# Six V blocks loaded in pairs: three 8 MB transfers with 64 KB rows, and fixed slots for K and V in a decode attention kernel

## The chip, the cores and the metric

The kernel runs on one core of a Trainium2 chip. The core has a matrix engine (PE, with its weight loads shown apart as PEld), VectorE (DVE), ScalarE (ACT), GpSimd (POOL) and SyncE (SP), which here only issues transfers. Sixteen DMA engines move data from the chip's main memory into the on-chip memory of 128 partitions; matrix products go to a second on-chip memory, PSUM, of eight banks. The metric is the device time of one execution in microseconds, lower is better.

## The reference

A batch of 8 tokens x (576 wide) goes through two branches, mixed by a gate g:

```python
g = sigmoid((x * gate_w).sum(-1, keepdims=True))
q = (x @ wq) as 32 heads of 128
k, v = last 2048 of 8192 keys of the caches, 16 heads, each used by 2 query heads
a = softmax(q k^T / sqrt(128)) v @ wo
b = gelu(layernorm(x) @ w1 + b1) @ w2 + b2
out = g * a + (1 - g) * b
```

All inputs are bf16. The part of the caches that is read is 8 x 16 x 2048 x 128 values for K and as many for V, 67 MB each; the weights add 20 MB. Each value is used for two query rows only, so there is little arithmetic per byte.

## The kernel before

**Units.** K and V are cut into 16 units of 4 MB each, n = 4g + i. A unit holds 32 of the 128 (batch, head) pairs (group g) and 512 of their 2048 keys (step i). On chip a unit is 128 partitions of one row of 32 KB: a pair j fills four partitions x, each with 128 keys. Since softmax doesn't ask for an order of keys, any assignment will do as long as K and V have the same.

**A K unit** (`k_unit`) is handled in four quarters: VectorE transposes a quarter in blocks of 32 x 32 (line 694, "tr", into one of two halves of KT), and PE multiplies it with the block-diagonal queries (line 712, "qk", eight matmuls into PSUM banks 0 to 3; all but every fourth are issued through the helper at line 175, so they are listed there). Bank 0 to 3 hold the mask before that, written by ScalarE (line 655). After the last quarter, `softmax` takes the maximum on VectorE (645, "mx"), turns it into the running bias ("nb", 647 or 649), and ScalarE takes the exponential (651) into P. `spread` transposes P on VectorE (669, "pt").

**A V unit** (`v_item`) copies the transposed P into a zeroed block-diagonal array, the spread P (743 on ScalarE and 744 on POOL, two copies each; "px"). PE multiplies it with V in 64 matmuls of 256 columns ("pv", lines 757 and 186, a loop with address registers), and VectorE adds the result to O with the correction for the new maximum ("o", 798 or 800). After each group of four units, VectorE and PE fold O into the final sums (803 to 811). There is one home for the spread P, so the copies for unit n wait until the product of unit n-1 has read it; the last unit uses KT, cleared by POOL (727).

**Transfers.** All large loads are issued by SP, in one order. The 32 KB slots of each partition are four and are taken in turn (1, 2, 0, 3) by the stream K0 K1 V0 K2 V1 K3 ... V14 V15 and then by w2 and wo. A load waits on SP until the slot's last user is done: for a K unit its four transposes, for a V unit its product. At the start wq lies in slot 0, w1 from slot 3 on. At the end come the bias, two thirds of w2, wo in two pieces and the rest of w2, accumulated by PE into the output bank.

**Order.** Every operation is put into a graph with `deps` (real waits on semaphores) and `after` (order of start only). A planner (`_Plan.schedule`) gives each operation a time from its `cost` and writes a fixed order for each engine; transfers follow a rate `DMA_BW` and a latency `DMA_LAT`. `keep_warm` is a filler: matmuls with zeros into a bank that is rewritten later.

The lines around the transfer and the product of a V unit:

```python
def take_slot():
    n = n_slot[0]
    n_slot[0] += 1
    return (1, 2, 0, 3)[n % ND]
...
deps = [d, o_u] + px_done[n] + [o_done.get(n - 2)]
after = pv_hist[-1:] + [qk_unit.get(n + 1)]
```

Of the kernel before, what the change touches and what calls it, by code (L numbers as in the profile page):

```python
# [6 lines left out]
BF = mybir.dt.bfloat16  # L7
F32 = mybir.dt.float32
# [30 lines left out]
class _Plan:  # L39

    DMA_BW = 428e3
    DMA_LAT = 1.8
    DMA_ISSUE = 0.35
# [18 lines left out]
    def schedule(self):  # L62
# [14 lines left out]
        while ready:  # L77
# [18 lines left out]
            if op.is_dma:  # L96
                eng_free[op.eng] = est + op.cost
                if op.nbytes < 65536:
                    op.t1 = est + 0.4 + self.DMA_LAT
# [93 lines left out]
def build_kernel(nc, A_x, A_k_cache, A_v_cache, A_wq, A_wo, B_x, B_w1, B_b1, B_w2, B_b2, gate_w, out):  # L193
# [12 lines left out]
    ND = 4  # L206
# [10 lines left out]
    JN = D // NJ  # L217
    BIG = 1.0e9
    x2 = A_x.rearrange("b s d -> (b s) d")
    out2 = out.rearrange("b s d -> (b s) d")  # L220

    with ExitStack() as es:
# [14 lines left out]
        req("ident", 128, BF)  # L237
        req("ones_bf", 512, BF)
        req("zeros_bf", 128, BF)
# [12 lines left out]
        req("maskhd", 4, F32)  # L252
        req("r8", 128, F32)
        req("idf8", 8, F32)
        req("dg", 16, F32)
        req("sel", 4 * 128, BF)
        req("sel4", 128, BF)
        req("cols", 16, F32)
        req("xT", 6 * 32, BF)
        req("yT", 6 * 32, BF)  # L260
        req("q4", 4 * 256, BF)
        req("qbd", 4 * 4 * 128, BF)
        req("b2", D, BF)
        req("uh", FCW, F32)
        req("v1", FCW, F32)
        req("hT", FT * 32, BF)
# [5 lines left out]
        req("gcol", 1, F32)  # L272
        req("on", 512, BF)
        req("O", 256, F32)
        req("EW", 512, F32)
        req("EV", 128, F32)
        req("oT", 512, BF)
        req("out_sb", JN, BF)
# [4 lines left out]
        over("vm", "uh", 0, 256, F32)  # L283
        over("x_sb", "PT", 0, D, BF)
# [76 lines left out]
        def slot(s):  # L361
            return RAW[:, s * DE:(s + 1) * DE]
# [226 lines left out]

        stream = [("K", 0), ("K", 1)]  # L590
        for vi in range(NL):
            stream.append(("V", vi))
            if vi + 2 < NL:
                stream.append(("K", vi + 2))
        HEAD = 2
# [10 lines left out]
        slot_free = [[o_qp], [], [], [o_hp]]  # L606
        o_px0 = add("pool", lambda e: e.memset(ptx_f, 0.0), deps=[o_qp, o_hp], name="ptx0", cost=4.5)
        n_slot = [0]
        tr_hist, qk_half = [], []
        qk_unit, qb_done = {}, {}  # L610
        pt_done, px_done, pv_done = {}, {-1: [o_px0]}, {}
        ex_done, nb_done, al_done, ss_done, o_done = {}, {}, {}, {}, {}
# [5 lines left out]
        def take_slot():  # L618
            n = n_slot[0]
            n_slot[0] += 1  # L620
            return (1, 2, 0, 3)[n % ND]

        def load_item(cache, nm, n):
            s = take_slot()
            g, i = divmod(n, 4)
            src = cache.rearrange("b h s d -> (b h) s d")[32 * g:32 * g + 32, S0 + KL * i:S0 + KL * i + KL, :].rearrange("j (x r) d -> j x (r d)", x=4)
            d = dma("sp", lambda e: e.dma_start(slot(s), src), "s%d" % s, 8 * W * Dh * 2, deps=slot_free[s], name="%s%d" % (nm, n), after=last_dma[-1:])
            last_dma.append(d)
            slot_free[s] = []
            return s, d  # L630

# [54 lines left out]
        def k_unit(n, s, d):  # L686
            g, i = divmod(n, 4)
            trs = []
            for rh in range(2):
                for hh in range(2):  # L690
                    m = 4 * n + 2 * rh + hh
                    kb = m % 2
                    deps = [d] + ([qk_half[m - 2]] if m >= 2 else [o_selp])
                    tr = add("dve", (lambda rh=rh, hh=hh, kb=kb: lambda e: e.transpose(bass.AP(arena_f, offset=foffs("KT") + kb * 2048, ap=[[AST // 2, 128], [1, 2048]]),  # L694
                                                                                      bass.AP(arena_f, offset=foffs("RAW") + s * SE + rh * (SE // 2) + 32 * hh, ap=[[AST // 2, 128], [64, 64], [1, 32]])))(),
                             deps=deps, name="tr%d_%d%d" % (n, rh, hh), cost=2.3, after=tr_hist[-1:] + ([mx_done.get(n - 1)] if rh + hh == 0 else []) + ([pt_done.get(n - 1)] if rh == 1 and n < NL - 1 else []))
# [4 lines left out]
                    if (rh, hh) == ((1, 1) if n == NL - 1 else (1, 0)):  # L701
# [13 lines left out]
                    if rh == 0 and hh == 0:  # L715
                        deps += qb_done[g] + [mask_done[n]]
                    qk = add("pe", qk_fn, deps=deps, name="qk%d_%d%d" % (n, rh, hh), cost=1.85, after=qk_half[-1:] + pv_hist[-1:])
                    qk_half.append(qk)
            qk_unit[n] = qk
            if n > 4 and n % 4 == 1:  # L720
# [3 lines left out]
            if n == NL - 1:  # L724
                o_kz.deps.append(qk)

        o_kz = add("pool", lambda e: e.memset(view("KT").bitcast(F32), 0.0), deps=[], name="ktx0", cost=4.5, prio=3)  # L727

        def v_item(n):
            s, d = load_item(A_v_cache, "dv", n)  # L730
            g, i = divmod(n, 4)
            if n == NL - 1:
                spread(n)
            ob_ = BK_OS[n % 2]
            px_at = aoffs("KT") if n == NL - 1 else PX
            px_free = [o_kz] if n == NL - 1 else [pv_done.get(n - 1), o_px0]
            px_done[n] = []
            for c in range(4):
                def fn(e, c=c):
                    dst = bass.AP(arena, offset=32 * c * AST + px_at + 32 * c, ap=[[AST, 32], [128, 64], [1, 32]])  # L740
                    src = bass.AP(arena, offset=32 * c * AST + aoffs("PT") + 2048 * (n % 2), ap=[[AST, 32], [32, 64], [1, 32]])
                    if px_engs[n][c] == "act":
                        return e.activation(out=dst, in_=src, func=ACTF.Copy)  # L743
                    return e.tensor_copy(dst, src)  # L744
                px_done[n].append(add(px_engs[n][c], fn, deps=[pt_done[n]] + px_free, name="qrx%d_%d" % (n, c), cost={"act": 1.8, "dve": 0.8, "pool": 2.4}[px_engs[n][c]], prio=5))

            if n == NL - 2:
                mx_done[n + 1].after.extend(op for op in px_done[n] if op.eng == "dve")
                o_kz.deps.extend(op for op in px_done[n] if op.eng == "dve")

# [30 lines left out]
            deps = [d, o_u] + px_done[n] + [o_done.get(n - 2)]  # L781
            after = pv_hist[-1:] + [qk_unit.get(n + 1)]
            if n >= NL - 2:
                after.append(keep_warm("warm_pv%d" % n, (10, 6)[n - NL], after, (ob_,), [o_u, o_done[n - 2]]))
            if n < NL - 1:
                pv = add("pe", lambda e: pv_looped(e, 64, 2, 6 if n < NL - 2 else 12), deps=deps, name="pv%d" % n, cost=8.2, after=after)
            else:
                pva = add("pe", lambda e: pv_looped(e, 48, 4, 14), deps=deps, name="pv%da" % n, cost=5.4, after=after)
# [4 lines left out]
            slot_free[s] = [pv]  # L793
            al = sm[:, n, 3:4]
# [77 lines left out]
        def k_item(n):  # L872
            s, d = load_item(A_k_cache, "dk", n)
            k_unit(n, s, d)

# [9 lines left out]
        for kind, i in stream:  # L885
            {"K": k_item, "V": v_item, "W": wo_all, "M": m2_chunk, "B": bias}[kind](i)

# [63 lines left out]
```

## Time and profile before

| | |
|---|---|
| median of 3 runs | 364.5 us (364.47 to 364.72) |
| profiled execution | 364.57 us, span 363.3 us |
| busy | PE 284.4 us (78%), VectorE 257.3 (71%), ScalarE 131.8 (36%), POOL 73.5 (20%) |
| read from main memory | 154.31 MB, mean 425 GB/s over the span |
| granted PE clock, mean | 0.92 |
| K and V loads | 32 of 4 MB, 26.4 us from issue to landing (median) |
| transposes of K (694) | 64 of 2288 ns |
| maximum (645), transposed P (669), exponential (651), mask (655) | 16 of 2292, 16 of 2274, 16 of 1967, 15 of 1873 ns |
| copies into the spread P | 28 of 1884 ns on POOL, 30 of 1906 ns on ScalarE, 6 of 686 ns on VectorE |

The page gives the busy time of each engine as a share of the span, the span in 40 slices, the transfers, the chain of work that ended last and the costliest groups of instructions by line. The busy share of PE is modelled from pipelined matmuls and includes fillers. In the views in order of time, a row has start, busy time, engine, line, operation, operands and, in brackets, the idle time before it with what ended it. A line of SP marked L627 is the issue of a K or V load.

### The profile page before, as it was taken

To read this page: it belongs to the slowest core of one execution; us is meant where nothing else is said; L and a number is where in the kernel's file an instruction comes from. 1 tells how busy PE (TensorE), PEld (TensorE's weight loads), DVE (VectorE), ACT (ScalarE), POOL (GpSimd) and SP (SyncE) were. 2 spreads that over 40 slices of the span, in tenths; PEclk is the share of its full clock that TensorE was granted. 3 is DMA by queue.
4 is the path that set the end of the run, shared out by engine and by line. 5 is a ranking of instruction groups with operands and counts; after the bars stand their busy time and mean duration, and the time that the engine had idled before them with its cause. 6 is when DMAs were issued, how large, how long until landed. Compare 5 with 4: busy or idle time off the path is not lost.

```text
span 363.3 us, 4428 instructions
## 1 busy us (share of the span) xinstructions
PE 284.4 (78%) x1842; PEld 126.6 (35%) x1381; DVE 257.3 (71%) x201; ACT 131.8 (36%) x117; POOL 73.5 (20%) x72
## 2 busy tenths in 40 slices
PE   0355554999897967997978949897969679978996
PEld 0110000436171703452432607170706034513763
DVE  0722978797978596959495878677695979498530
ACT  1012106274544440735342434444444416313300
POOL 9123002230414040302212030404040403003000
PEclk9976596999998997999896998998999899999999
DMA  8999999999999999999999999999999999999995
GB/s 349 433 440 402 462 404 459 404 462 404 462 404 460 404 462 408 456 411 451 413 451 415 451 415 451 415 451 413 447 419 451 415 451 412 449 415 447 412 440 234
DMA packets 6146, 154.45 MB, mean 425 GB/s; under 512 B 716, under 2 KB 884, under 8 KB 1272
## 3 DMA queue, kind: packets, MB, share of 16 engines
q1 hardware_dynamic: 6080, 154.29, 98.7%
q8 instruction: 6, 0.10, 0.1%
q10 hardware_dynamic: 56, 0.03, 0.0%
q14 instruction: 4, 0.03, 0.0%
HBM read 154.31 MB, written 0.01 MB: 425 GB/s over the span
## 4 chain that ended last, share of the span: by engine, by line
DMA 50%; DVE 35%; PE 9%; issue 4%; ACT 2%; ACTq 0%; POOL 0%; SPq 0%
DMA arena<-in_A_k_cache_dram 42%; DVE arena L694 20%; DMA arena<-in_B_w_dram 5%; DVE arena L669 5%; PE ps L175 4%; DMA arena<-in_gate_w_dram 2%; DVE arena L645 2%; PE ps L186 2%; DVE arena L803 1%; PE ps L505 1%; PE ps L712 1%; DVE arena L800 1%; DVE arena L566 1%; DVE arena L808 1%; ACT arena L651 1%
## 5 line engine op out<-in xcount | busy, mean ns | idle before, releaser
L694 DVE STREAM_TRANSPOSE arena<-arena 128x2048 f32<-128x2048 f32 x64 | 145.0, 2288 | 23.6 <-DMA arena<-in_A_k_cache_dram 20.9
L175 PE MATMUL ps<-arena 128*128 128x512 bf16 (+2 forms) x461 | 131.2, 436 | 0.0
L186 PE MATMUL ps<-arena 128*128 x942 | 106.1, 274 | 0.1
L712 PE MATMUL ps<-arena 128*128 128x512 bf16 x128 | 54.6, 426 | 54.4 <-DVE arena L694 47.7
L186 PEld LDWEIGHTS ps<-arena 128*128 x942 | 92.4, 98 | 11.6 <-issue 0.6
L744 POOL COPY arena<-arena 32x2048 bf16<-32x2048 bf16 x28 | 52.8, 1884 | 211.1 <-DVE arena L669 210.3
L743 ACT ACTIVATE arena<-arena 32x2048 bf16<-32x2048 bf16 x30 | 57.2, 1906 | 64.3 <-DVE arena L669 64.0
L651 ACT ACTIVATE arena<-ps,arena 128x2048 bf16<-128x2048 f32 x16 | 31.5, 1967 | 113.1 <-DVE arena L649 78.5
L712 PEld LDWEIGHTS ps<-arena 128*128 128x128 bf16 x128 | 13.5, 105 | 159.0 <-DVE arena L694 98.1
L645 DVE TENSOR_REDUCE arena<-ps 128x1 f32<-128x2048 f32 x16 | 36.7, 2292 | 35.4 <-PE ps L175 35.4
L669 DVE STREAM_TRANSPOSE arena<-arena 128x2048 bf16<-128x2048 bf16 x16 | 36.4, 2274 | 2.1 <-ACT arena L651 2.1
L655 ACT ACTIVATE ps<-arena 128x2048 f32<-128x2048 f32 x15 | 28.1, 1873 | 0.1
L757 PE MATMUL ps<-arena 128*128 128x256 bf16 x82 | 14.5, 276 | 1.0 <-DVE arena L744 1.0
L757 PEld LDWEIGHTS ps<-arena 128*128 128x128 bf16 x82 | 8.0, 100 | 19.0 <-issue 17.1
L455 PE MATMUL ps<-arena 8*128 8x8 bf16 x8 | 0.6, 171 | 14.6 <-DVE arena L429 9.5
L583 PE MATMUL ps<-arena 128*8 128x288 bf16 (+1 forms) x140 | 9.6, 286 | 1.6 <-DMA arena<-in_A_wo_dram 0.6
L561 DVE TENSOR_TENSOR arena<-arena 128x1152 f32<-128x1152 f32 x1 | 1.4, 1358 | 11.5 <-ACT arena L559 11.5
L727 POOL MEMSET arena<- 128x4096 f32 x1 | 3.5, 3510 | 22.7 <-DVE arena L744 22.7
L583 PEld LDWEIGHTS ps<-arena 128*8 128x8 bf16 (+1 forms) x140 | 5.7, 86 | 5.9 <-DMA arena<-in_B_w_dram 1.3
L638 POOL COPY arena<-arena 32x128 bf16<-32x128 bf16 x16 | 4.6, 287 | 15.0 <-ACT arena L540 7.4
L429 DVE COPY arena<-arena 8x64 bf16<-8x64 bf16 x2 | 0.3, 190 | 9.1 <-DMA arena<-in_gate_w_dram 9.1
L800 DVE SCALAR_TENSOR_TENSOR arena<-arena,ps 128x256 f32<-128x256 f32 x12 | 5.3, 446 | 1.4 <-PE ps L757 1.4
(106 smaller groups left out, 98.9 us busy)
## 6 DMA issues: line engine op xcount, KB each, us to landing
arena<-in_A_k_cache_dram SPq DMA_DIRECT2D x16, 4096.0 KB, 26.4
arena<-in_A_v_cache_dram SPq DMA_DIRECT2D x16, 4096.0 KB, 26.3
arena<-in_B_w_dram SPq DMA_DIRECT2D x1, 4608.0 KB, 23.3
arena<-in_A_wo_dram SPq DMA_DIRECT2D x2, 2304.0 KB, 20.6
arena<-in_A_wq_dram SPq DMA_DIRECT2D x1, 4096.0 KB, 12.9
arena<-in_B_w_dram SPq DMA_DIRECT2D x1, 3456.0 KB, 26.6
arena<-in_B_w_dram SPq DMA_DIRECT2D x1, 1152.0 KB, 19.6
arena<-in_B_w_dram SPq DMA_DIRECT2D x1, 576.0 KB, 24.2
```

The costliest lines, as they stand in the source:

```text
L175: return e.add_instruction(mybir.InstMatmult(name=nc.get_next_instruction_name(), engine=mybir.EngineType.PE, ins=[e.lower_ap(rhs), e.lowe ...
L186: return e.add_instruction(mybir.InstMatmult(name=nc.get_next_instruction_name(), engine=mybir.EngineType.PE, ins=[operand(r, r_ap), opera ...
L583: ins = e.matmul(ps[32 * j:32 * j + 8, BK_ACC, 0:JN], lhsT, rhs[:, JN * j:JN * j + JN], start=False, stop=True, skip_group_check=True, til ...
L645: mx = mx_done[n] = add("dve", lambda e: e.tensor_reduce(out=k(n, MX), in_=ps[:, 0:4, :].rearrange("p a n -> p (a n)"), axis=AXL.X, op=ALU ...
L651: ex = add("act", lambda e: e.activation(out=Pm, in_=ps[:, 0:4, :].rearrange("p a n -> p (a n)"), func=ACTF.Exp, bias=k(n, NB), scale=SCAL ...
L655: mask_done[n + 1] = add("act", lambda e: e.activation(out=ps[:, 0:4, :].rearrange("p a (n c) -> p (a n) c", c=32), in_=bass.AP(arena_f, o ...
L669: pt_done[n] = add("dve", lambda e: e.transpose(bass.AP(arena, offset=aoffs("PT") + 2048 * (n % 2), ap=[[AST, 128], [1, 2048]]), Pm), deps ...
L694: tr = add("dve", (lambda rh=rh, hh=hh, kb=kb: lambda e: e.transpose(bass.AP(arena_f, offset=foffs("KT") + kb * 2048, ap=[[AST // 2, 128], ...
L712: mm = e.matmul(*args, start=False, stop=True, skip_group_check=True) if rc == 0 else held_matmul(nc, e, *args, stop=True, skip=True)
L743: return e.activation(out=dst, in_=src, func=ACTF.Copy)
L744: return e.tensor_copy(dst, src)
L757: mm = e.matmul(ps[:, ob_, 0:256], lhsT, rhs, start=(k == 0), stop=True, skip_group_check=True)
```

## The change

1. The stream is written out: K0 K1 V0 K2 V1 K3 V2 K4 V3 K5 K6 P4 K7 K8 P6 K9 K10 P8 K11 K12 V10 V11 K13 V12 K14 V13 K15 V14 V15. P4, P6 and P8 load V4 with V5, V6 with V7 and V8 with V9 in one transfer of 8 MB, with 64 KB for each partition. For that, units 2m and 2m+1 share a stretch of 1024 keys, 256 to a partition, and each takes one half of the 256. A single load, K or V, still has rows of 32 KB, which now lie 64 KB apart within one pair.
2. K uses slot 1 for even units and slot 0 for odd ones, V slot 2 for even and 3 for odd ones; a pair fills 2 and 3 and waits until both are free. The loads after the stream take slots 1, 0 and 2.
3. The spread P has two homes, the old one and PXB (which the gelu's temporaries use before), each cleared once by POOL; a copy for unit n waits for the product of n-2. KT is not used for it any more. Small arrays are laid over others to make room.
4. In the K unit after the second of a pair's (6, 8, 10, and 15 as before) P of the unit before is transposed after all four quarters instead of after the second. The product of a pair's first V unit comes after the scores of unit n+2 instead of n+1.
5. Ahead of the scores of units 6, 8 and 10 PE runs a filler of 16 matmuls with zeros, written as a loop.
6. The product loops of the last two V units have bodies of 6 instead of 12 and 14 matmuls; the planner's numbers are changed.

```diff
-    DMA_BW = 428e3
-    DMA_LAT = 1.8
+    DMA_BW = 433.2e3
+    DMA_LAT = 0.45
+    DMA_START = 1.7
...
-                    start = max(est + 0.4, dma_free)
+                    start = max(est + self.DMA_START, dma_free)
...
+    STREAM = "K0 K1 V0 K2 V1 K3 V2 K4 V3 K5 K6 P4 K7 K8 P6 K9 K10 P8 K11 K12 V10 V11 K13 V12 K14 V13 K15 V14 V15"
...
+        req("PXB", SE, BF)
+        over("uh", "PXB", 0, FCW, F32)
+        over("v1", "PXB", 4 * FCW, FCW, F32)
...
-        ptx_f = bass.AP(arena_f, offset=PX // 2, ap=[[AST // 2, 128], [1, 4096]])
+        PXS = (PX, aoffs("PXB"))
...
+        px_zero = [add("pool", (lambda k=k: lambda e: e.memset(bass.AP(arena_f, offset=PXS[k] // 2, ap=[[AST // 2, 128], [1, 4096]]), 0.0))(), deps=[o_qp, o_hp] + [o_hf] * k, name="ptx%d" % k, cost=4.5) for k in range(2)]
+        late_slots = [1, 0, 2]
+        pairs = [int(k[1:]) for k in STREAM.split() if k[0] == "P"]
+        late_turn = [n + 2 for n in pairs] + [NL - 1]
...
-        def load_item(cache, nm, n):
-            s = take_slot()
+        def load_item(cache, nm, n, s, both=False):
             g, i = divmod(n, 4)
-            src = cache.rearrange("b h s d -> (b h) s d")[32 * g:32 * g + 32, S0 + KL * i:S0 + KL * i + KL, :].rearrange("j (x r) d -> j x (r d)", x=4)
+            keys = cache.rearrange("b h s d -> (b h) s d")[32 * g:32 * g + 32, S0 + 2 * KL * (i // 2):S0 + 2 * KL * (i // 2) + 2 * KL, :]
+            if both:
+                src, dst = keys.rearrange("j (x r) d -> j x (r d)", x=4), RAW[:, s * DE:(s + 2) * DE]
+            else:
+                src, dst = keys.rearrange("j (x u r) d -> u j x (r d)", x=4, u=2)[n % 2], slot(s)
+            free = slot_free[s] + (slot_free[s + 1] if both else [])
...
-                    if n and (rh, hh) == ((1, 1) if n == NL - 1 else (0, 1)):
+                    if n and (rh, hh) == ((1, 1) if n in late_turn else (0, 1)):
                         spread(n - 1, after=[tr])
+                    if (rh, hh) == (0, 1) and n - 3 in pairs and n - 3 in o_done:
+                        o_done[n - 3].after.append(tr)
...
+                        if n - 2 in pairs:
+                            qk_half.append(keep_warm("warm_qk%d" % n, 16, qk_half[-1:] + pv_hist[-1:], (BK_OS[n % 2],), [o_u, nb_done[n - 1], o_done[n - 4]], looped=True))
...
+        def v_pair(n):
+            d = load_item(A_v_cache, "dv", n, 2, both=True)
+            for u in range(2):
+                v_unit(n + u, 2 + u, d)
...
-            px_at = aoffs("KT") if n == NL - 1 else PX
-            px_free = [o_kz] if n == NL - 1 else [pv_done.get(n - 1), o_px0]
+            px_at = PXS[n % 2]
+            px_free = [pv_done.get(n - 2), px_zero[n % 2]]
...
-            after = pv_hist[-1:] + [qk_unit.get(n + 1)]
+            after = pv_hist[-1:] + [qk_unit.get(n + 2 if n in pairs else n + 1)]
...
-                pv = add("pe", lambda e: pv_looped(e, 64, 2, 6 if n < NL - 2 else 12), deps=deps, name="pv%d" % n, cost=8.2, after=after)
+                pv = add("pe", lambda e: pv_looped(e, 64, 2, 6), deps=deps, name="pv%d" % n, cost=7.1, after=after)
...
-        def keep_warm(name, n, after, banks=(0, 1, 2, 3), deps=None):
+        def keep_warm(name, n, after, banks=(0, 1, 2, 3), deps=None, looped=False):
             def fn(e):
                 mm = None
+                if looped:
+                    args = (ps[:, banks[0], :], zeros_bf, maskR)
+                    e.matmul(*args, start=True, stop=True, skip_group_check=True)
+                    with e.Fori(0, n - 2):
+                        held_matmul(nc, e, *args, start=True, stop=True, skip=True)
+                    return held_matmul(nc, e, *args, start=True, stop=True, skip=True)
...
         def k_item(n):
-            s, d = load_item(A_k_cache, "dk", n)
-            k_unit(n, s, d)
+            s = 1 - n % 2
+            k_unit(n, s, load_item(A_k_cache, "dk", n, s))
```

More of the change, by code (lines that the diff above doesn't have):

```diff
@@ L237, in build_kernel @@
         req("ident", 128, BF)
-        req("ones_bf", 512, BF)
+        req("EW", 512, F32)
+        over("ones_bf", "EW", 0, 512, BF)
+        over("sel", "EW", 1024, 4 * 128, BF)
         req("zeros_bf", 128, BF)
@@ L252, in build_kernel @@
         req("maskhd", 4, F32)
-        req("r8", 128, F32)
         req("idf8", 8, F32)
         req("dg", 16, F32)
-        req("sel", 4 * 128, BF)
         req("sel4", 128, BF)
         req("cols", 16, F32)
-        req("xT", 6 * 32, BF)
-        req("yT", 6 * 32, BF)
+        req("early", 640, BF)
+        over("xT", "early", 0, 6 * 32, BF)
+        over("yT", "early", 384, 6 * 32, BF)
+        over("r8", "early", 768, 128, F32)
+        over("b2", "early", 0, D, BF)
         req("q4", 4 * 256, BF)
         req("qbd", 4 * 4 * 128, BF)
-        req("b2", D, BF)
-        req("uh", FCW, F32)
-        req("v1", FCW, F32)
+        req("vm", 256, F32)
+        req("PXB", SE, BF)
+        over("uh", "PXB", 0, FCW, F32)
+        over("v1", "PXB", 4 * FCW, FCW, F32)
         req("hT", FT * 32, BF)
@@ L282, in build_kernel @@
         req("RAW", ND * DE + SE, BF, 512)
-        over("vm", "uh", 0, 256, F32)
+        over("on", "P", 0, 512, BF)
+        over("oT", "P", 1024, 512, BF)
+        over("out_sb", "PT", 0, JN, BF)
         over("x_sb", "PT", 0, D, BF)
@@ L587, in __init__ @@
                 acc_groups.append(self)
[L590 to L594, printed above, removed]
+        stream = [(k[0], int(k[1:])) for k in STREAM.split()]
         HEAD = 2
@@ L618, in take_slot @@
         def take_slot():
[L619 to L627 removed]
+            return late_slots.pop(0)
+        def load_item(cache, nm, n, s, both=False):
+            g, i = divmod(n, 4)
+            keys = cache.rearrange("b h s d -> (b h) s d")[32 * g:32 * g + 32, S0 + 2 * KL * (i // 2):S0 + 2 * KL * (i // 2) + 2 * KL, :]
[4 more added lines that the diff above has]
+            free = slot_free[s] + (slot_free[s + 1] if both else [])
+            d = dma("sp", lambda e: e.dma_start(dst, src), "s%d" % s, (1 + both) * 8 * W * Dh * 2, deps=free, name="%s%d" % (nm, n), after=last_dma[-1:])
             last_dma.append(d)
             slot_free[s] = []
[L630 removed]
+            if both:
+                slot_free[s + 1] = []
+            return d
         def query(g):
@@ L716, in k_unit @@
                         deps += qb_done[g] + [mask_done[n]]
-                    qk = add("pe", qk_fn, deps=deps, name="qk%d_%d%d" % (n, rh, hh), cost=1.85, after=qk_half[-1:] + pv_hist[-1:])
+                        if n - 2 in pairs:
+                            qk_half.append(keep_warm("warm_qk%d" % n, 16, qk_half[-1:] + pv_hist[-1:], (BK_OS[n % 2],), [o_u, nb_done[n - 1], o_done[n - 4]], looped=True))
+                    qk = add("pe", qk_fn, deps=deps, name="qk%d_%d%d" % (n, rh, hh), cost=1.75, after=qk_half[-1:] + pv_hist[-1:])
                     qk_half.append(qk)
+                    kt_free.append(qk)
             qk_unit[n] = qk
-            if n > 4 and n % 4 == 1:
+            if n > 4 and n % 4 == 1 and (n - 5) // 4 in us_done:
                 us_done[(n - 5) // 4].after.append(qk)
```

33 lines of the change are left out of this document (12 added, 21 removed).

## The prediction

> **What bounds the kernel now.** I read the page first (span, slices, chain), then the stretches between two arrivals of K, then the waits of SP, which issues every large transfer, then SP, PE and VectorE in order of time around K5 and K6.
>
> ```profile
> span 363.3 us, 4428 instructions
> ...
> DMA  8999999999999999999999999999999999999995
> ...
> HBM read 154.31 MB, written 0.01 MB: 425 GB/s over the span
> ...
> DMA 50%; DVE 35%; PE 9%; issue 4%; ACT 2%; ACTq 0%; POOL 0%; SPq 0%
> ```
>
> The DMA engines are full in every slice but the first and the last. The chain names VectorE for 35%, but that is the way back from one arrival of K to the instruction that issued a transfer. Whether the engines ever run dry is seen between arrivals of K (start and end, length, PE busy, granted clock, DMA share, GB/s):
>
> ```profile
> 124.50:163.20 38.70, 31.40 (x191) 0.91 1.00 433
> 163.20:201.90 38.70, 32.83 (x184) 0.87 1.00 433
> 201.90:240.60 38.70, 32.90 (x209) 0.96 1.00 433
> ...
> 344.00:355.00 11.00, 10.28 (x114) 1.00 1.00 427
> ```
>
> And what SP waited for (us in total, times, longest):
>
> ```profile
> SPq L627 <- DVE arena L694: 114.8, 12, 17.3
> ...
> SPq L898 <- DMA out_dram<-arena: 1.1, 1, 1.1
> ```
>
> Four transfers of 4.19 MB take 38.7 us at share 1.00 and 433 GB/s. SP waits a lot (a K transpose, L694, frees a slot), yet nobody behind it starves: a transfer lands 26.4 us after its issue (page, last part) and needs 9.7 of its own, so it was queued some 16.7 us early. So the time is: about 1 us until the first byte, 154.3 MB at 433 GB/s (356.4 us), some 2 us of slack at start and in the 430s of single stretches, 3.7 us from the last landing (359.6) to the end (363.3), and 1.3 us outside the span (the profiled execution took 364.57; the median of the runs is 364.5). No byte is taken away by the change. It can only gain through a higher rate, and lose through an empty DMA queue. The sum is therefore a list of deadlines for SP's issues.
>
> The last row above is SP's only wait for a transfer into an idle queue: 0.32 us of issue and 1.1 of wait, 1.42 us from issue to landing for 4.5 KB. I use it as the price of a start from an empty queue.
>
> **The work around the first pair, as it runs now.** PE in order of time (the bracket is the idle time before, and who ended it):
>
> ```profile
> 133.47 0.40 PE L712 MATMUL ps<-arena 128*128 128x512 bf16 x1 [2.41 <-DVE arena L694]
> ...
> 138.85 0.61 PE L712 MATMUL ps<-arena 128*128 128x512 bf16 x1 [2.99 <-DVE arena L694]
> ...
> 142.84 0.38 PE L757 MATMUL ps<-arena 128*128 128x256 bf16 x2
> ...
> 149.82 0.39 PE L712 MATMUL ps<-arena 128*128 128x512 bf16 x1
> ```
>
> VectorE, then SP, then the clock of that stretch:
>
> ```profile
> 142.18 2.29 DVE L645 TENSOR_REDUCE arena<-ps 128x1 f32<-128x2048 f32 x1 [3.39 <-PE ps L175]
> ...
> 151.82 2.31 DVE L694 STREAM_TRANSPOSE arena<-arena 128x2048 f32<-128x2048 f32 x1 [0.55 <-PE ps L175]
> ```
>
> ```profile
> 126.41 0.54 SPq L627 DMA_DIRECT2D arena<-in_A_v_cache_dram  x1
> ```
>
> ```profile
> 130.00:140.00 10.00, 4.59 (x16) 0.74 1.02 439
> ```
>
> Read off: one V unit holds PE 6.98 us (142.84 to 149.82), and its slot is reissued 7.18 us after its first matmul (119.23 to 126.41). A quarter of scores holds PE 1.80 us (149.82 to the next at 151.62), and the transpose that waits for it starts 2.0 us after the quarter's start (149.82, 151.82). Transposes follow each other every 2.2 us. The granted clock fell to 0.74 over 130 to 140, after idle gaps of 2.41 and 2.99 us, and the quarter at 138.85 took 3.1 instead of 1.8.
>
> **Part by part.** *Rows of 64 KB.* Each of 16 engines moves 8 rows per 4 MB; six units go from 48 rows to 24. Price per row: wo's rows of 18 KB ran at 427 GB/s in the stretch above, K and V at 433 with 32 KB; a fixed cost that explains it is 22 ns per row (18,432 B at 26.69 B/ns is 691 ns, 32,768 at 27.06 is 1,211; the line through both meets zero bytes at 22), so 24 x 22 = 0.5 us gained at most. The stretch 345 to 355, with the same rows of 18 KB, shows 433, so the other end is 0. I take 0.1, near the second, since edges cut a stretch by whole packets. The K rows stay at 32 KB, now 64 KB apart within a head; a head's stride stays 2 MiB, so I cost this at nothing.
>
> *Slots.* K has slots 1 and 0, V has 2 and 3. The order up to K5 is unchanged, so times up to K5's arrival (124.52) can be kept. Arrivals after it, at 9.70 us each (318.46 minus 124.52 is 193.94 for 20 transfers): K6 134.2, P4 153.6, K7 163.3, K8 173.0, P6 192.4, K10 211.8. A transfer costs nothing if issued 1.42 us before its predecessor lands. K2 now waits for K0's transposes (50.42; deadline about 54), P4 for PV of V3 (126.41; deadline 132.8), K8 for K6's transposes (155.2 below; deadline 161.9). They hold by 3.5, 6.4 and 6.7 us. P6 and P8, which need both V slots, are left.
>
> *P6.* Deadline 171.6 (K8 lands 173.0). Start at VectorE's maximum of K5, as now 142.18 to 144.47, bias 144.66. K6 landed at 134.2, so its first two transposes run as in the trace, 144.6 to 149.0. The new filler, 16 matmuls, starts at 144.66 and takes 3.7 us (nine took 2.10 us at 329.44), to 148.4; the mask of K6, on ScalarE as now, is written at 148.7, and covers it. Today K6's scores waited for the PV of V4 until 149.82; that PV now comes later. Quarter one 148.75; third transpose 150.75, fourth 152.95 to 155.15; last quarter 155.2; PV of V4 at 157.0 (P4 landed 153.6, its spread P is old). P of V5 is transposed 155.15 to 157.4 and copied by POOL and ScalarE (two each, 1.9 us a copy) until 161.3, into its second home; PV of V5 starts at 164.0, so it is not held. Slot 3 is free and P6 issued at 164.0 + 7.2 = 171.2. That is 0.4 us inside the deadline: cost 0.
>
> *P8.* Deadline 210.4 (K10 lands 211.8). K7's scores stand behind both PV on PE: 171.0; third transpose 173.0, the update of O 0.4, fourth 175.6 to 177.8, last quarter 177.85, maximum 179.9 to 182.2, exponential and mask 4.0 after 182.5 (161.25 to 165.26 in the trace) to 186.5, the filler meanwhile from 182.35 to 186.1; K8's quarters and transposes 186.5, 188.5, 190.7, 192.95; PV of V6 194.75 (P6 landed 192.4), PV of V7 201.75, P8 issued 208.9: 1.5 us inside. V10 needs only the PV of P8's first half, and its own start is two K loads after P8's landing (231.2), so it has 19 us for 7. What each wait holds up: behind P6 on SP are K9 and K10, due 19 us later.
>
> *The rest.* The three fillers hide under the mask; without that cover each costs 3.7 us on PE. POOL clears two homes for P (3.51 us each) early and no longer clears KT at 332.20: POOL has 290 us idle, and the last PV waits for VectorE's copies (339.07 on), not for it: 0. Bodies of 6 instead of 12 and 14 in the last two PV loops: 60 matmuls took 6.71 us in the one form and 6.72 in the other: 0. Tail: the M2 slot now comes from K14 (earlier), wo's first from K15 as before, its second from V14 as before (issued 339.9, and it is queued behind 8 us of w2): 0. Fewer waits for spread P: 0, since DMA sets the pace.
>
> Sum: 364.57 - 0.1 + 0 = 364.47 for a profiled execution, and 0.07 less for a median: 364.4 us.
>
> **A rule weighed.** The granted clock of K6's quarters decides P6. In the trace it dropped after gaps of 2.41 and 2.99 us. The Trainium skill, "TensorE: Matmul & The Clock Gate", section on what is actually happening, says that half rate comes after at least one idle window of about 3.4 us; by that rule the 1.8 to 2.7 us of idle PE ahead of the fillers would never halve the clock, and the sum would be 364.4. The trace differs (2.99 us, clock 0.74) and decides: by it the first rival's 366.7 is open too.
>
> **Rivals.** *P6 starts late (slower).* The slack is 0.4 us in a chain of 47 us. If the filler runs at half clock (a matmul of 512 columns then takes 0.42 us, four in 1.68 from 138.85), it lasts 6.7 us to 151.4 instead of 148.4, K6's first quarter moves from 148.75 to 151.4, and P6 is issued at 173.85: 2.25 us of empty engines, 366.7. The same ahead of K8 adds 2.65 - 1.5 = 1.2: 367.9. It decides from 0.4 us on; at 1.2 it is over the bound. For it: the measured drop, and a chain with no idle time. Against it: PE was back at full clock from 142 on in the trace, just before the filler. Chance 0.33.
>
> *The long rows pay (faster).* 22 ns per row, 0.5 us: 364.0, and with half a microsecond more from fewer completions or instruction fetches under 363.8. Against it: share 1.00 at 433 in every stretch. Chance of more than 0.2%: 0.08.
>
> *The address pattern costs rate (slower).* Rows of 64 KB keep each engine longer in one place, and the heads lie 2 MiB apart. At 427 instead of 433 GB/s, the slowest stretch, 25.2 MB cost 58.9 instead of 58.1 us: 365.2. The trace shows the 2 MiB stride at the full 433 with rows of 32 KB. Chance 0.04. The Trainium skill, "DMA: Bandwidth & Descriptors", section on latency and other measured facts, gives 164 GB/s for a row pitch of 2 MiB; estimated from that page, 25.2 MB would take 153 us. The trace (433 at that pitch) does not agree, so it moves no chance.
>
> *The change does nothing that shows* is my forecast, 0.55.
>
> **How the numbers follow.** This kernel's runs agree within 0.25 us, so 0.2% (0.7 us) is what a measurement can tell. Forecast 364.4; its own range is 364.0 (rows at their best) to 365.2 (P6 0.8 late). Low 363.9. The rival's 366.7 has most of what is slower, so high is 367.0; some 0.1 lies above and under 0.1 below. Faster 0.08, same 0.55, slower 0.37 (0.33 + 0.04).
>
> **What the profile after would show.** Right: share 1.00 and 433 GB/s across 165 to 215, P6 issued near 171 and P8 near 209, last landing near 359.5, PV of V4 and V5 back to back on PE. Wrong: a dip in the GB/s slice at 171 to 175, with SP released by PE after 171.6; L175 matmuls of the filler at 0.42 us; K7 arriving on time but K9 late by the same amount as P6. If the share stays 1.00 and the time still moves, the rate of 64 KB rows is the cause.

## The result, and the profile after

The changed kernel takes 370.6 us (median of 6 runs, 367.96 to 372.05) against 364.5 (364.38 to 364.72): a ratio of 1.0161, 95% interval 1.0143 to 1.0178. It is slower, by 6 us, above the top of my range (367.0). The spread of its runs grew from 0.3 us to 4. The profiled execution took 370.06 us.

The page of the kernel after:

```profile
span 368.8 us, 4559 instructions
...
DMA  8999999999999999998999999999999999999994
...
HBM read 154.31 MB, written 0.01 MB: 418 GB/s over the span
...
DVE 42%; PE 36%; DMA 14%; ACT 4%; issue 3%; ACTq 0%; POOL 0%; SPq 0%
```

The bytes are the same, the rate over the span fell from 425 to 418 GB/s, one slice in the middle fell from 9 to 8, and in the chain the DMA engines gave way to PE (9% to 36%). So the transfers had waited for the arithmetic. Where, the same stretches show (start and end, length, PE busy, granted clock, DMA share, GB/s):

```profile
124.50:163.20 38.70, 30.35 (x148) 0.96 1.00 433
163.20:201.90 38.70, 33.89 (x204) 1.00 0.97 409
201.90:240.60 38.70, 31.78 (x180) 1.00 0.97 409
240.60:279.50 38.90, 34.22 (x231) 0.96 1.00 433
279.50:318.50 39.00, 32.83 (x201) 0.96 1.00 433
```

At 409 instead of 433 GB/s a stretch of 38.7 us loses 38.7 x (1 - 409/433) = 2.15 us. Two such stretches make 4.3 of the 5.5 us by which the span grew. Outside them the rate is the old one, with rows of 64 KB as with rows of 32. The rest is at the end: the same length of time, 3.8 us before the end of the span, in the kernel after and then in the one before:

```profile
340.00:365.00 25.00, 23.50 (x243) 1.00 0.94 402
```

```profile
334.50:359.50 25.00, 22.82 (x239) 1.00 0.98 418
```

That is 25 x 16/433 = 0.9 us more. The issues of the two pairs, on SP:

```profile
171.19 0.54 SPq L631 DMA_DIRECT2D arena<-in_A_v_cache_dram  x1
...
210.60 0.54 SPq L631 DMA_DIRECT2D arena<-in_A_v_cache_dram  x1
```

P6 was issued at 171.19; the prediction worked out 171.2. It was still late: the engines ran dry around it, as a short stretch of the kernel after shows (the last column is GB/s). P8 was issued 1.7 us after the 208.9 worked out.

```profile
171.00:172.00 1.00, 1.00 (x7) 1.00 0.08 33
```

PE around the filler ahead of K6, in order of time (line 176 is the helper that was 175, 720 the scores, 838 the filler's first matmul, 770 and 187 a product):

```profile
143.36 0.39 PE L838 MATMUL ps<-arena 128*128 128x512 bf16 x1 [1.72 <-DVE arena L655]
143.59 5.22 PE L176 MATMUL ps<-arena 128*128 128x512 bf16 x15
148.65 0.39 PE L720 MATMUL ps<-arena 128*128 128x512 bf16 x1
...
157.03 0.38 PE L770 MATMUL ps<-arena 128*128 128x256 bf16 x2
...
171.00 0.39 PE L720 MATMUL ps<-arena 128*128 128x512 bf16 x1
```

The 16 matmuls hold PE from 143.36 to 148.65, 5.3 us, 0.33 a matmul. Then come K6's scores, and from 157.03 to 171.00 the two products, back to back. K7's scores, whose data VectorE had begun to transpose at 163.1, start only after them. VectorE shows what that did to it: what the transposes waited for (us in total, times, longest), before and then after:

```profile
DVE arena L694 <- DMA arena<-in_A_k_cache_dram: 20.9, 10, 3.5
DVE arena L694 <- PE ps L175: 2.8, 3, 1.2
```

```profile
DVE arena L700 <- PE ps L176: 19.4, 9, 3.3
DVE arena L700 <- DMA arena<-in_A_k_cache_dram: 10.5, 5, 3.3
```

Before, VectorE waited for data; now it mostly waits for PE to read one of the two halves of KT.

### The profile page after: what moved, and what is told of

It is laid out like the page before. It is cut to its first block, busy times and chain, and to the rows that moved or that the text cites. A ratio compares the mean times of both kernels' runs of the same rounds, so it can differ in the third digit from the quotient of the medians.

```text
span 368.8 us, 4559 instructions
## 1 busy us (share of the span) xinstructions
PE 290.0 (79%) x1875; PEld 124.4 (34%) x1384; DVE 261.0 (71%) x201; ACT 131.7 (36%) x117; POOL 73.6 (20%) x72
## 4 chain that ended last, share of the span: by engine, by line
DVE 42%; PE 36%; DMA 14%; ACT 4%; issue 3%; ACTq 0%; POOL 0%; SPq 0%
DVE arena L700 24%; PE ps L187 15%; PE ps L176 14%; DMA arena<-in_A_k_cache_dram 7%; DMA arena<-in_B_w_dram 5%; DVE arena L651 5%; DVE arena L675 4%; PE ps L720 3%; DMA arena<-in_gate_w_dram 2%; ACT arena L657 1%; PE ps L509 1%; ACT arena L757 1%; PE ps L770 1%; DVE arena L816 1%; DVE arena L813 1%
## 5 line engine op out<-in xcount | busy, mean ns | idle before, releaser
L176 PE MATMUL ps<-arena 128*128 128x512 bf16 (+2 forms) x496 | 138.3, 414 | 10.9 <-DVE arena L700 8.3
L187 PE MATMUL ps<-arena 128*128 x942 | 107.9, 275 | 0.2
L187 PEld LDWEIGHTS ps<-arena 128*128 x942 | 91.1, 99 | 14.8 <-issue 2.1
L720 PE MATMUL ps<-arena 128*128 128x512 bf16 x124 | 49.9, 402 | 37.2 <-DVE arena L700 29.0
L720 PEld LDWEIGHTS ps<-arena 128*128 128x128 bf16 x128 | 12.8, 100 | 159.1 <-DVE arena L700 88.8
L770 PEld LDWEIGHTS ps<-arena 128*128 128x128 bf16 x82 | 7.9, 100 | 14.9 <-issue 13.1
L607 POOL MEMSET arena<- 128x4096 f32 x2 | 7.0, 3512 | 10.0 <-DVE arena L569 5.5
```

Of the source, the lines that this page charges most:

```text
L176: return e.add_instruction(mybir.InstMatmult(name=nc.get_next_instruction_name(), engine=mybir.EngineType.PE, ins=[e.lower_ap(rhs), e.lowe ...
L187: return e.add_instruction(mybir.InstMatmult(name=nc.get_next_instruction_name(), engine=mybir.EngineType.PE, ins=[operand(r, r_ap), opera ...
L720: mm = e.matmul(*args, start=False, stop=True, skip_group_check=True) if rc == 0 else held_matmul(nc, e, *args, stop=True, skip=True)
L770: mm = e.matmul(ps[:, ob_, 0:256], lhsT, rhs, start=(k == 0), stop=True, skip_group_check=True)
```

## The experiments

The first theory after the result: the price is the **joint wait** of a pair for both V slots, so the same order with single loads would be back at the old time. Its rival was the **order** itself: two K and then two V make the chain of PE and VectorE over four units longer than the four transfers of 38.7 us, so that loads come too late whichever way they are cut. The first two runs set these against each other. All edits are against the changed kernel, whose times are 370.6 us and 1.0161.

**e1: the same order of work, single loads.** The V units come one by one; fillers, order on every engine and all else are kept.

```diff
-    STREAM = "... K5 K6 P4 K7 K8 P6 K9 K10 P8 K11 ..."
+    STREAM = "... K5 K6 V4 V5 K7 K8 V6 V7 K9 K10 V8 V9 K11 ..."
...
-        pairs = [int(k[1:]) for k in STREAM.split() if k[0] == "P"]
+        pairs = [4, 6, 8]
```

> The order of transfers and of all engines stays that of the changed kernel; only P4, P6 and P8 become two transfers of 4 MB, each waiting for its own slot. Theory A (a pair must wait for both V slots, so P6 and P8 are issued when the DMA queue has run empty): V6 waits only for the product of V4, which ends near 164, 7 us before the slot of V5, so it is issued near 164 and the queue never runs dry; DMA share 1.00 throughout 164 to 216; 364.3 to 365.5. Theory B (two K loads followed by two V loads make the work of PE and VectorE longer than the transfers, as the chain of the changed kernel with PE 36% and DVE 42% suggests): stays at 368 to 371.

369.7 us (368.44 to 371.61), ratio 1.0126 [1.0104, 1.0147]. The joint wait isn't the whole price. Without it V6 is issued at 165.62 and the stretch of 163.2 to 201.9 is back at 431 GB/s, but nearly all of the loss stays, only elsewhere. SP in order of time and three short stretches of e1:

```profile
138.71 18.42 SPq L631 DMA_DIRECT2D arena<-in_A_k_cache_dram  x2
...
179.34 18.39 SPq L631 DMA_DIRECT2D arena<-in_A_k_cache_dram  x2
...
223.13 17.60 SPq L631 DMA_DIRECT2D arena<-in_A_k_cache_dram  x2
```

```profile
235.00:240.00 5.00, 4.39 (x19) 1.00 0.80 347
240.00:245.00 5.00, 4.78 (x37) 1.00 0.74 269
326.00:334.00 8.00, 7.39 (x50) 1.00 0.80 311
```

A row of two issues begins with K7, K9 and K11 in turn. From one to the next are 40.6 and 43.8 us, 84.4 together, where eight transfers take 77.4: nothing waits for two slots here, and still the chain falls 7 us behind. One round above 38.7 us is no lag by itself: in the kernel before the same three issues come at 138.82, 174.66 and 216.17, which is 35.8 and 41.5 us, 77.3 together. In e1 the engines run dry at 235 to 245, when K12 waits (issued at 240.2) for the transposes of K10, and again at 326 to 334, when V15 waits (issued at 329.6) for a product. That is 2.9 and 2.2 us of the 7.0 by which the span of e1 (370.3 us) is longer than that of the kernel before.

**e2: two 4 MB loads that wait as one.** As e1, but the first of two V loads waits for both slots. Rows are 32 KB.

```diff
-            free = slot_free[s] + (slot_free[s + 1] if both else [])
+            free = slot_free[s] + (slot_free[3] if nm == "dv" and n in pairs else [])
```

> As the changed kernel, but a pair is two transfers of 4 MB with rows of 32 KB; the first waits for both V slots, as the pair does. Theory A1 (the lateness of the issue is the whole price, whatever the rows): V6 is issued near 171, the dips at 170 to 175 and 211 to 216 stay, 369 to 371. Theory A2 (rows of 64 KB and a single issue make the restart dearer: the first rows of P6 and P8 are slow): the dips shrink by about half, 366 to 368.

371.6 us (370.24 to 373.19), 1.0193 [1.0157, 1.0229]. V6 was issued at 172.66, and the stretch of 163.2 to 201.9 fell to 394 GB/s. With the wait of the pairs but not their rows, the loss is that of the pairs: the 64 KB rows are not to blame.

**e3: no fillers.**

```diff
-                        if n - 2 in pairs:
+                        if False:
```

> The changed kernel without the three fillers. In the changed kernel a filler takes 5.3 us (143.36 to 148.65) where 3.7 were expected, and ends 1.3 us after the mask (147.36) that should cover it. Theory F1 (the fillers hold PE): scores of K6, K8 and K10 begin 1.3 us earlier each, P6 is issued near 169.9, and 1.3 to 3 us are won: 367 to 369. Theory F2 (without them the clock falls to half in the scores and the products that follow): P6 is issued later than 171.2 and the time is 371 or more.

372.2 us (370.39 to 372.36), 1.0191 [1.0163, 1.0218]. PE in order of time, the clock of the filler's stretch (then the first stretch with a loss), and P6 on SP:

```profile
149.51 0.58 PE L720 MATMUL ps<-arena 128*128 128x512 bf16 x1 [5.01 <-ACT ps L661]
149.89 1.48 PE L176 MATMUL ps<-arena 128*128 128x512 bf16 x3
```

```profile
143.00:157.00 14.00, 8.99 (x24) 0.69 0.97 417
163.20:201.90 38.70, 30.38 (x190) 0.91 0.88 373
```

```profile
174.25 0.54 SPq L631 DMA_DIRECT2D arena<-in_A_v_cache_dram  x1
```

Without the filler PE is idle for 5.01 us, the granted clock over this stretch is 0.69 (1.00 in the changed kernel), three matmuls of K6's scores take 1.48 instead of 0.84 us, and P6 is issued 3.1 us later. Not all of that is the filler's: already ahead of its place, K5's last quarter ran at half clock in this execution (0.50 over 138 to 143), and K5's maximum started at 142.83, 2.0 us later than in the changed kernel. The medians of e3 and of the changed kernel are 1.6 us apart and their ranges overlap. What a filler is worth is clearer against e8, whose shorter one gives 367.75.

**e4: the product of the first V unit ahead of the second K's scores.**

```diff
-            after = pv_hist[-1:] + [qk_unit.get(n + 2 if n in pairs else n + 1)]
+            after = pv_hist[-1:] + [qk_unit.get(n + 1 - (n % 2) if n - n % 2 in pairs else n + 1)]
```

> The changed kernel, but the products of a pair need not stand behind the second K's scores on PE: the planner may put them where the pair lands. Theory A: P6 is issued before 171, by up to 3 us, and the loss falls by what the issue is earlier: 365.5 to 369. Theory B: the scores of K6, K8 and K10 come later instead, no change or slower, 370 or more.

370.4 us (369.52 to 371.43), 1.0161 [1.0137, 1.0185]. Inconclusive: the planner, free to move the product, still put it behind K6's scores (at 157.96), so the order asked for did not come about. P6 was issued at 172.12 and its stretch ran at 395 GB/s, a further point for the price below.

**e5: the rest of the change alone.** The old alternating order, hence no pairs and no fillers; fixed slots, two homes of spread P, layout of keys, loop bodies and planner numbers stay.

```diff
+    STREAM = "... K5 V4 K6 V5 K7 V6 K8 V7 K9 V8 K10 V9 K11 V10 K12 V11 K13 ..."
```

> The changed kernel with the old alternating order of K and V, no pair, no filler; the fixed slots (K 0 and 1, V 2 and 3), the two homes of spread P, the new planner numbers and the shorter loop bodies stay. Theory C (the order of two K and two V makes a chain on PE and VectorE that is longer than the four transfers: K5, K7 and K9 gave their slot free at 138.7, 179.3 and 223.1 in the first run, 40.6 and 43.8 us apart, against 38.7 for four transfers): with the order gone the time is that of the kernel before, 364.2 to 365.2. Theory D (the fixed slots or another part of the rest cost time): above 366.

364.8 us (364.66 to 365.24), 1.0003 [0.9994, 1.0013]. All that I had costed at nothing costs nothing.

**e6: one pair (P4), then alternating.**

```diff
+    STREAM = "... K5 K6 P4 K7 K8 V6 V7 K9 V8 K10 V9 K11 V10 K12 V11 K13 ..."
```

> Only P4 stays a pair, in the same place; after it K7 K8 V6 V7 and then the alternating order in single transfers. P4 itself was issued on time in the changed kernel (125.69), so this has rows of 64 KB with no late issue, and one round of the order of two and two. Theory C: the first round alone costs little, since the chain starts it with slack; 364.3 to 366. Rows of 64 KB by themselves: at most 0.1 us won, not to be seen. If rows of 64 KB cost rate, the stretch of P4 shows less than 433 GB/s.

364.8 us (364.69 to 365.13), 1.0003 [0.9993, 1.0012]. One pair costs nothing and gains nothing: in the stretch that its 8 MB arrive in, 124.5 to 163.2, the rate is 433 GB/s, as before. With one pair the chain falls behind once, within the slack that queued loads give.

**e7: the changed kernel with shorter products.** Pairs, 64 KB rows, waits and fillers stay; 30 of 64 key pieces of the products of V4 to V9 are left out.

```diff
-                pv = add("pe", lambda e: pv_looped(e, 64, 2, 6), ...)
+                pv = add("pe", lambda e: pv_looped(e, 34 if 4 <= n < 10 else 64, 2, 6), ...)
```

> The changed kernel with 34 instead of 64 matmuls in the products of V4 to V9: 30 of the 64 pieces of the keys of these units are left out of the output. Nothing else changes, every wait and every transfer stays. Theory C: a pair holds PE 6.5 us less, P6 and P8 are issued near 165 and 201, the share is 1.00 throughout, and with the long rows alone left the time is 364.2 to 365.5. If the pairs cost time for a reason on the transfer's side (restart, rows of 64 KB, the wait for two slots as such): 367 or more.

364.7 us (364.55 to 366.31, 10 runs), 1.001 [0.9997, 1.0022]. The issues of P6 and P8, and the two stretches:

```profile
166.64 0.54 SPq L631 DMA_DIRECT2D arena<-in_A_v_cache_dram  x1
...
202.50 0.54 SPq L631 DMA_DIRECT2D arena<-in_A_v_cache_dram  x1
```

```profile
163.20:201.90 38.70, 32.87 (x178) 0.91 1.00 432
201.90:240.60 38.70, 28.10 (x124) 0.91 1.00 434
```

P6 is issued 4.6 and P8 8.1 us earlier, both dips are gone and with them the loss. All transfers and all waits of the change are there, so the loss is the length of the chain on PE, through the issue times.

**e8: a filler of 10, written out,** instead of 16 in a loop.

```diff
-... keep_warm("warm_qk%d" % n, 16, ..., looped=True))
+... keep_warm("warm_qk%d" % n, 10, ...))
```

> The changed kernel with fillers of 10 matmuls written out instead of 16 in a loop. They take about 2.3 us instead of 5.3 and end before the mask, so each K after a pair starts its scores 1.3 us earlier. If the clock stays up as with the long filler, P6 is issued near 170, P8 two to three us earlier, and 2 to 3 us are won: 366.5 to 368.5. If the long filler was needed for the clock: 370 or more, as without a filler.

367.75 us (367.31 to 368.38), 1.009 [1.0073, 1.0107]. PE, the stretches, and P6 and P8 of e8:

```profile
144.63 2.10 PE L176 MATMUL ps<-arena 128*128 128x512 bf16 x9
...
148.53 0.39 PE L720 MATMUL ps<-arena 128*128 128x512 bf16 x1 [1.80 <-ACT ps L661]
```

```profile
163.20:201.90 38.70, 32.51 (x213) 1.00 0.97 412
201.90:240.60 38.70, 31.27 (x186) 0.96 1.00 434
```

```profile
171.07 0.54 SPq L631 DMA_DIRECT2D arena<-in_A_v_cache_dram  x1
...
209.06 0.54 SPq L631 DMA_DIRECT2D arena<-in_A_v_cache_dram  x1
```

The ten take 2.3 us, keep the clock, and end before the mask. Half of the loss is gone: P8 comes at 209.06, close to the 208.9 of the prediction, and the second dip is gone. The first dip stays, because P6 is where it was: in this execution K5's last quarter ran in part at half clock (0.50 over 141 to 143), K5's maximum started at 141.86 instead of 140.82, and what the shorter filler won ahead of K6 was lost there (scores from 148.53 instead of 148.65).

**e9: the price of a late start by itself.** Alternating order as in e5, and one load, V6, also waits for the end of V5's unit.

```diff
+            free = slot_free[s] + ([o_done[5]] if (nm, n) == ("dv", 6) else [])
```

> The alternating kernel of the run before (364.8 us, never an empty queue), in which the single load of V6 waits for one thing more: VectorE's update of O for unit 5, which ends at 172.8 there. V6's turn comes at the same place as P6's (after K5 V4 K6 V5 K7, so K7's... predecessor lands at 173.0). Nothing else is late. It measures the price of a start from an empty queue by itself. By the prediction's price (an issue 1.42 us ahead of the predecessor's landing costs nothing, deadline 171.6): 1.2 us lost, 366.0. By the line through the five runs with a late P6 or V6 (issued at 171.07, 171.19, 172.12, 172.66, 174.25, stretches without a full queue and slow first rows together 1.6, 2.2, 3.2, 3.6, 5.3 us; deadline near 169.0): 3.8 us lost, 368.5, and a single transfer with rows of 32 KB pays the same.

378.3 us (378.07 to 378.89), 1.0374 [1.0357, 1.0391]. V6 was issued at 172.40. The expectation placed V6 one transfer too late: its predecessor is K7, whose first transpose starts at 163.06. The DMA engines around it in e9 (the columns of the stretches):

```profile
159.00:161.00 2.00, 2.00 (x21) 1.00 0.72 311
161.00:162.00 1.00, 1.00 (x11) 1.00 0.39 164
162.00:172.40 10.40, 7.84 (x52) 1.00 0.00 0
172.40:173.00 0.60, 0.60 (x4) 0.63 0.00 0
173.00:176.00 3.00, 2.77 (x8) 0.51 0.80 273
```

The engines don't finish together: 159 to 162 loses 3 - (2 x 311 + 164)/433 = 1.2 us. The landing is known 1.06 us after the last byte (162 to 163.06). Nothing arrives in the first 0.6 us after the issue, and the next 3 us run at 273 GB/s, 1.1 us lost. Together 4.0 us: to cost nothing, this load had to be issued 4.0 us before its predecessor was seen to land, not 1.42. The whole run says the same: 172.40 - (163.06 - 4.0) = 13.3 us, measured 378.26 - 364.77 (e5) = 13.5; by 1.42 it would be 10.8.

The other runs give the same price (edges of short stretches cut whole packets, so the four parts are good to some tenths). K8 was due at 173.0; the loss is 38.7 x (1 - GB/s/433) in the stretch of 163.2 to 201.9:

| run | load after K8 issued at | GB/s | lost, us | issued minus lost |
|---|---|---|---|---|
| e7 | 166.64 | 432 | 0.1 | |
| e8 | 171.07 | 412 | 1.9 | 169.2 |
| after | 171.19 | 409 | 2.15 | 169.0 |
| e4 | 172.12 | 395 | 3.4 | 168.7 |
| e2 (32 KB rows) | 172.66 | 394 | 3.5 | 169.2 |
| e3 | 174.25 | 373 | 5.4 | 168.9 |

The last column is the deadline, 169.0 within 0.3: 4.0 us before 173.0. Behind K10 the price is less sharp: counted in the same way, with K10 due as much later than 211.8 as the first stretch lost, the second stretch asks for a lead of 5.5 us in the changed kernel, 5.1 in e2, 4.8 in e3 and 4.6 in e4. So 4.0 is what P6 paid, and P8 paid somewhat more.

**e10: single loads (e1) with the short filler (e8).**

> Order of two K and two V, single transfers, fillers of 10 matmuls written out. Theory C (the chain on PE and VectorE over four units against 38.7 us): with the long filler the singles lost 5 us, because the chain took 40.6 and 43.8 us a round; the short one takes some 1.5 us out of each round and no V waits for two slots, so nearly all of the loss goes: 364.7 to 366.0. If the wait for both slots and not the chain's length were what is left of the loss with short fillers (367.75), it would be 364.7 as well; if the order costs for another reason, 367 or more.

365.45 us (364.9 to 367.67, 10 runs), 1.0032 [1.0012, 1.0052]. K7, K9 and K11 are 38.5 and 41.2 us apart (139.15, 177.65, 218.84), 79.7 together, against 84.4 in e1 and 77.3 in the kernel before. The second round is no longer than before; what is left of the lag comes from the first. To come within 1 us of the old time, both the single loads and the short filler are needed:

| median, us | filler of 16 in a loop | filler of 10 written out |
|---|---|---|
| pairs | 370.6 | 367.75 |
| single loads | 369.7 | 365.45 |

The long filler costs 2.9 us more than the short one with pairs and 4.3 with single loads. The pairs cost 2.3 us with the short filler; with the long one the 0.9 between the medians lies within overlapping ranges. They don't add; that both draw on the same few us by which loads are issued early is argued, not shown. In the profiled execution of e10 (366.76 us, one of its slower ones) every stretch from 124.5 to 318.5 runs at 431 GB/s or more. The lag is carried to the end of the stream: V15 is issued at 324.8, in e5 at 321.2, and the rate drops there, in e10 and then in e5:

```profile
324.00:332.00 8.00, 7.11 (x34) 1.00 0.97 393
324.00:332.00 8.00, 7.51 (x33) 1.00 1.01 434
```

That is 0.7 us of the 1.8 by which the span of e10 is longer than that of e5; where the rest goes is open.

**e11: two pairs (P4, P10) with alternating units between them.**

```diff
+    STREAM = "... K5 K6 P4 K7 K8 V6 V7 K9 V8 K10 V9 K11 K12 P10 K13 K14 V12 V13 K15 V14 V15"
```

> Two pairs, P4 and P10, with alternating rounds in between, so that the chain can catch up before the next pair; fixed slots, two homes and long fillers stay. Theory C: no pair is issued into an empty queue, share 1.00 throughout, 364.5 to 365.3. If rows of 64 KB won something, each pair would show at most 0.1 us; not to be told from zero here.

366.05 us (364.7 to 367.2, 10 runs), 1.0028 [1.0014, 1.0042], above what was expected. From 235 to 245 the rate is 360 GB/s, while K12 waits for K10's slot: between the pairs the chain had not caught up. No version of the change is faster than the kernel before.

## Why the prediction was wrong, step by step

- **The frame held.** The time moved only through an empty DMA queue; the rate of full stretches stayed 433 GB/s. But the list of deadlines was wrong in three terms.
- **The price of a start (mis-sized, and this decides P6).** "A transfer costs nothing if issued 1.42 us before its predecessor lands" took the 4.5 KB output as the row for a load of 8 MB. Measured: 4.0 us at P6 (1.2 + 1.06 + 0.6 + 1.1 in e9, 169.0 against 173.0 in the table). The output moves 4.5 KB only; it can't show that sixteen engines finish at different times and fill up slowly. With 4.0, the step's own 171.2 against a deadline of 169.0 gives 2.2 us lost; measured 2.15. The Trainium skill, "DMA: Bandwidth & Descriptors", section "Anatomy of one DMA", gives about 2.0 us of fixed cost to a transfer, for the GpSimd path. Taken as the lead this would be an estimate of 171.0 for the deadline and 0.2 us lost; the runs of the table do not agree.
- **P6 at 171.2 (right, by two errors).** The filler takes 5.3 us, not 3.7: the price came from a filler that is written out (0.23 us a matmul), while this one is a loop with one matmul a turn (0.33, at clock 1.00). So "The three fillers hide under the mask" fails; K6's mask was written at 147.36, and the filler ended 1.3 us later. But K5's last quarter ran at full clock in this execution, so the maximum came at 140.82 instead of 142.18, and K6's scores start at 148.65 as worked out (148.75).
- **P8 at 208.9, 1.5 us inside (wrong).** With the long filler 210.60, with one of 2.3 us 209.06 (e8): the filler's term is most of this step's error. The table's line gives some 0.7 us for it (K10 due at 211.8 + 2.15, less 4.0, is 209.95), the stretch shows 2.15. About 1.4 us there stays unexplained, and e2, e3 and e4 show 0.6 to 1.1 us of the same; that the engines finish even less together after the first gap is only argued.
- **"P6 and P8 are left" (incomplete).** I checked issues one by one up to P8 and never added up a whole round against 38.7 us. In e1 two rounds take 84.4 us where the transfers take 77.4. What makes them long is that PE takes in two products in 14 us, during which VectorE can only fill two halves of KT, and the filler: with shorter products the two rounds go from 81.8 (the changed kernel) to 79.5 us (e7), with the shorter filler from 84.4 (e1) to 79.7 (e10). The fold of O after a group, which I did not cost either, falls into K9's round; but it does so in the kernel before too, where that round takes 41.5 us without harm. So later loads are late too (K12 in e1 and e11, V15 in e1 and e10).
- **64 KB rows, 0.1 of at most 0.5 us.** No gain measured: 364.80 with one pair (e6) and 364.73 with all three but shorter products (e7), against 364.73. The rival of the long rows, and that of the address pattern, fall. The 164 GB/s that the prediction took from the Trainium skill ("DMA: Bandwidth & Descriptors", section "Latency and other measured facts") was measured on copies between tensors in main memory, in rows of 16 KiB; the 433 GB/s here, for loads into on-chip memory in rows of 32 KB, don't contradict it, though the prediction read them so.
- **The rest, 0.** Right (e5: 1.0003 [0.9994, 1.0013]).
- **"P6 starts late" (0.33).** The right sign for a mechanism that was not at work: the filler ahead of K6 ran at clock 1.00 (143 to 157), as did both stretches with a loss, and K6's scores ran at half clock only without the filler (e3). On that gate, "TensorE: Matmul & The Clock Gate" of the Trainium skill, section "What's actually happening", asks for an idle window of about 3.4 us; the 1.72 us ahead of the filler kept the clock and K6's scores ran at 0.50 after the 5.01 us of e3, as it says. The kernel before differs, though by another gap than the prediction named: its clock fell from 1.00 to 0.50 at about 135, after the gap of 2.41 us and ahead of the one of 2.99. The same gap of 2.41 us, in the same place, left the clock at 1.00 in e1 (134 to 138), so its length alone does not decide.

Open: the 0.9 us of the last stretch (402 against 418 GB/s), the 1.4 us at P8, and the spread of 4 us. That the lag is near the edge, so that a quarter at full or half clock decides in each execution, fits K5's maximum (140.82 in the changed kernel, 141.86 in e8, 142.83 in e3) but was not shown, with one profiled execution of each.

## What to carry to other kernels

Where the DMA queue sets the time, add up the arithmetic of whole rounds of slots, two in a row (84.4 us in e1, 77.3 in the kernel before), and compare it with the transfers of these rounds (77.4); checking single issues hides a lag that grows, and a single round can be too long without harm. Price a late issue by a large load that really started from an empty queue, since the lead that it needs was nearly three times that of a small transfer here (4.0 against 1.42 us). Price a filler by its own form: a loop of single matmuls is not the straight run of the same number.

## What the runs showed that I had not expected

- A 4 or 8 MB load from an empty queue needs its issue 4.0 us before the predecessor is seen to land (behind K8, five runs within 0.3 us, and 13.5 us lost in e9 where this gives 13.3), with rows of 32 and of 64 KB alike; behind K10 the same runs ask for 4.6 to 5.5.
- A loop with one 128x512 matmul a turn takes 0.33 us a matmul at full clock, a straight run 0.23.
- Rows of 64 KB move at the 433 GB/s of rows of 32 KB.
- One gap of 2.41 us on PE, in the same place, was followed by half clock in the kernel before and by full clock in e1.
